# First samples in two pieces, with zero products between them, and another order of taps and weight sums, in a two-convolution transducer joint

## The chip, the cores and the metric

The kernel runs on one core of one Trainium2 chip. The metric is the device time of one execution in microseconds (us). A profile is one further execution of the same program. Its page and its trace count time from the first instruction of the program, and the span is the time from there to the end of the last one.

## The reference, cut to what matters

```python
B, T, D, K, U = 2, 4000, 512, 5, 8          # all inputs bf16
xp = pad(x, 2 samples of zeros at both ends of T)
h = sum(einsum("btc,cd->btd", xp[:, i:i+T, :], w1[i]) for i in range(K))
h = gelu(h)[:, ::2, :]                      # 2000 samples are kept
hp = pad(h, 2 at both ends)
f = sum(einsum("btc,cd->btd", hp[:, i:i+2000, :], w2[i]) for i in range(K))
f = gelu(f)[:, ::2, :]                      # 1000 samples are kept
fe, ge = f @ w_f, g @ w_g
j = tanh(fe[:, :, None, :] + ge[:, None, :, :])   # (2, 1000, 8, 512)
out = j @ w_o                               # bf16
```

The change touches the very start: the first convolution over the first samples of batch 0, and the sums of its weights that the rest of the convolution needs.

## The kernel before, in words

A small planner writes the program. Each operation is recorded with its engine, what it reads and writes and an estimated cost (`Plan.op`, `Plan.dma`). `schedule` then plays the operations through in time and settles the order in which each engine issues them, and `learn` repeats that up to `PASSES` times with other priorities, and keeps the best plan. Engines run their lists strictly in order and wait on semaphores. TensorE (PE) takes the ready operation that was recorded first; ScalarE (ACT) and VectorE (DVE) take the one with the least slack. All loads are issued by SyncE (SP), in the order of the record.

The work has these stages.

**Direct part.** For the first 444 kept samples of h in batch 0 the convolution is done tap by tap. `load_xr` brings the rows of x in, 128 partitions with two consecutive samples each (an even and an odd one), in four pieces `xr`: three of 256 KB and one of 128 KB. PE transposes each piece (lines 573 to 588): for each of the two phases, four 128x128 transposes into one PSUM bank. ACT copies the even phase, DVE the odd phase, into `eo`, which holds two phases of samples with channels on partitions. Then `direct(i)` (line 744) does the five taps in the order of `TAPS`, 16 products of 444 columns each: four output groups `m` of 128 channels, four slices of input channels. Even taps read the even phase of `eo`, odd taps the odd phase. The four groups accumulate in PSUM banks 0, 2, 4 and 6. While the first piece is on its way, `NWARM` products of zeros run on PE (`warm_mm`, line 565).

**Triple part.** The rest of the first convolution and all of the second one are done by `Triple` and `Unit`. Three neighbouring outputs are computed with nine products in place of fifteen, from sums and differences of samples (`row`, `xa`, `xp`) and of weights. The samples come by transposing DMAs (`load_x6`, line 513), six phases to a buffer. The weight sums are made by `w1part(m)` (line 612) for each of the four groups: seven sums on DVE, most with 512 elements on each partition, and three scaled copies on ACT. Groups m and m+2 share the scratch buffers `wu`, `ssum` and `ws`, so that group 2 can't be begun before group 0 has used them.

**Joint part.** `fe`, `ge`, tanh on ACT, and the last product with `w_o`, partly by a seven-product scheme (`Seven`), with stores by SP.

The order of SP's list at the start is: four `xr` pieces, tap 0 of `w1`; tap 2 (which waits until the third piece has landed); tap 4 (waits for the fourth piece); two transposing loads into `xa`; tap 1 (waits for tap 0); one `xa` load; tap 3 (waits for tap 2); three `xa` loads; then eighteen `xp` loads. The waits come from `came[-3]` in lines 535 to 541: a load may be issued when the third load before it in that list has landed.

Of the kernel before, what the change touches and what calls it, by code (L numbers as in the profile page):

```python
# [68 lines left out]
class Plan:  # L69
# [1 line left out]

    COMPUTE = ("pe", "act", "dve", "pool")
    HOP = 0.16
    PASSES = 100

    def __init__(self, nc):
        self.nc = nc
# [277 lines left out]
def bass_standalone__seq2seq_rnn_t_joint__speech_kernel(  # L355
# [22 lines left out]
    NK = D // P  # L378
# [3 lines left out]
    ND, NF = 444, 184  # L382
    NL = 2 * NT3 - ND // 3 - NF
    assert ND % 6 == 0 and NF % 2 == 0 and NL % 2 == 0
    EW = 464
    XW = 528
    HOFF, HWID = 2, 338
    JB = 2 * P
    RING, WIDE, XB = 12, 10, 24
    BU = B * U  # L390
    NT = 512
    NWARM = 5
    TAPS = (0, 2, 4, 1, 3)
    XR = [P] * ((ND + 1) // P) + [32 * -(-((ND + 1) % P) // 32)]
    NX = len(XR)

    with ExitStack() as es:
# [18 lines left out]
        wo_sb = at("wo_sb", [NK, D], BF16)  # L416
        h_off = cur[0]
        hT = [at(f"hT{b}", [6, NK, HWID], BF16) for b in range(B)]
        wu = [Buf(nc, f"wu{i}", [NK, P], FP32, h_off + 24576 + i * 2048) for i in range(2)]
        xr = [Buf(nc, f"xr{i}", [2, NK, P], BF16, h_off + 16384 + i * 2048) for i in range(NX)]  # L420
        assert hT[0].end <= h_off + 16384 and xr[-1].end <= h_off + 24576 and wu[1].end <= cur[0]
        sd = [at(f"sd{i}", [3, 336], FP32) for i in range(3)]
        ws = [at(f"ws{i}", [NK, P], FP32) for i in range(2)]
        ssum = [at(f"ssum{i}", [NK, P], FP32) for i in range(2)]
        geT = at("geT", [NK * BU], FP32)
        gT = at("gT", [NK, BU], BF16)
        zero = at("zero", [NT], BF16)
        ident = at("ident", [P], BF16)
# [1 line left out]
        xe = at("xe", [NK, 16], BF16)  # L430
        assert cur[0] <= 229368, cur[0]
        eo = Buf(nc, "eo", [2, NK, EW], BF16, w2_sb.end - w2_sb.bytes)
        assert eo.end <= w2_sb.end and 16 + sum(XR) <= EW
        xa = Buf(nc, "xa", [7, NK, 224], BF16, xs[0].end - xs[0].bytes)
        assert xa.end <= xs[0].end
        xp = [Buf(nc, f"xp{i}", [6, NK, 352], BF16, xs[i].end - xs[i].bytes) for i in range(3)]
        assert all(a.end <= b.end for a, b in zip(xp, xs))
        w1_x = Buf(nc, "w1_x", [3, NK, D], BF16, wf_sb.end - wf_sb.bytes)
# [34 lines left out]
        def tt(eng, o, a, b, op):  # L473
            pl.op(eng, lambda e: e.tensor_tensor(out=o.ap, in0=a.ap, in1=b.ap, op=op), (a, b), (o,),  # L474
                  0.02 + 2.14e-3 * o.ap.free_size() if eng == "pool" else vec_cost(o, (a, b)))

        def act(o, i, func, scale=1.0, bias=None):
            rd = (i,) if bias is None else (i, bias)
            pl.op("act", lambda e: e.activation(o.ap, i.ap, func, scale=scale,  # L479
                                                bias=0.0 if bias is None else bias.ap), rd, (o,),  # L480
                  o.ap.free_size() * 0.833e-3 + (0.05 if i.psum else 0.105 if bias is None else 0.186))

        def mm(o, pairs, start, stop, check=True):

            def fn(e):
                for n, (l, r) in enumerate(pairs):
                    ins = e.matmul(o.ap, lhsT=l.ap, rhs=r.ap, start=start and n == 0,  # L487
                                   stop=stop and n == len(pairs) - 1, skip_group_check=not check)
                return ins
            pl.op("pe", fn, [v for pr in pairs for v in pr], (o,), len(pairs) * max(o.ap.free_size() / 2400 + 0.0025, 0.1))  # L490


        zv = zero[:]
# [4 lines left out]
            out=idv.ap, in_=zero[0:P].ap, compare_op=ALU.not_equal, fill=1.0, base=0,  # L498
# [6 lines left out]
            return pl.dma(eng, lambda e: e.dma_start(dst.ap, src), (), (dst,), slack=slack)  # L505

        def load_xr(rt):
            n = XR[rt]
            dst = xr[rt].rows(0, n, slice(0, 2)).map(lambda a: a.rearrange("p r k c -> p (r k c)"))
            src = x[0, 2 * P * rt:2 * (P * rt + n), :].rearrange("(p r) c -> p (r c)", r=2)  # L510
            return pl.dma("sp", lambda e: e.dma_start(dst.ap, src), (), (dst,), nbytes=2048 * n)  # L511

        def load_x6(buf, b, ph, j0, col, n=336, slack=1.0):

            r0 = b * T + 6 * j0 + ph
            dst = buf[ph, :, col:col + n]
            src = x.rearrange("b t d -> (b t) d")[r0:r0 + 6 * (n - 1) + 1:6, :]
            return pl.dma("sp", lambda e: e.dma_start_transpose(out=dst.ap, in_=src), (), (dst,), nbytes=n * 2 * D, rate=175e3, slack=slack)  # L518
# [10 lines left out]
        JA, JL = ND // 3 - 1, (ND // 3 + NF) - 1  # L529

        def load_a(*phs):
            for ph in phs:
                load_x6(xa, 0, ph, JA, 0, 16 * -(-(NF + 2) // 16), 0.0)

        came.append(load_w1(TAPS[0]))
        for i in TAPS[1:3]:
# [7 lines left out]
        memset(xp[1][:, :, 336:340])  # L544
        pl.pin = False
        for ph in (4, 0, 2, 1, 3, 5):
            load_x6(xp[1], 0, ph, JL, 0, slack=0.3)
            if ph > 3:
                memset(xp[1][ph, :, 335:336])
        pl.pin = True  # L550
# [14 lines left out]
        def warm_mm(lo, hi):  # L565
            z, zz = zero[0:P], zero[:]
            for i in range(lo, hi):
                mm(ps.cols((2 * i + 1) % 8 * NT, NT), [(z, zz)], True, True)
                pl.ops[-1].cost = 0.43

        warm_mm(0, NWARM)
        psb = ps.h[:, :].bitcast(BF16)
        for rt in range(NX):
            for r in range(2):
                bk = (4 * rt + 2 * r) % 8
                n = XR[rt]
                pv = View(psb[:, bk * 1024:bk * 1024 + NK * n].rearrange("p (k c) -> p k c", k=NK), np.array([bk]), True)

                def fn(e, rt=rt, r=r, pv=pv, n=n):
                    for k in range(NK):  # L580
                        ins = e.transpose(pv.ap[:, k, :], xr[rt].h[0:n, r, k, :], ident.h[0:n, 0:n])
                    return ins
                pl.op("pe", fn, (xr[rt][:], ident[:]), (pv,), 0.43)
                o = eo[r, :, 16 + rt * P:16 + rt * P + n]
                if r == 0:
                    act(o, pv, ACT.Copy)
                else:
                    pl.op("dve", lambda e, o=o, pv=pv: e.tensor_copy(out=o.ap, in_=pv.ap), (pv,), (o,), vec_cost(o, (pv,)))

        def stt(eng, o, a, f, b):  # L590
            pl.op(eng, lambda e: e.scalar_tensor_tensor(  # L591
                out=o.ap, in0=a.ap, scalar=f, in1=b.ap, op0=ALU.mult, op1=add), (a, b), (o,),
                  vec_cost(o, (a, b), False))
# [18 lines left out]
        def w1part(m):  # L612
            sl = slice(m * P, (m + 1) * P)
            w = lambda i: w1_sb[i, :, sl]
            u, v, t = wu[m % 2][:], ssum[m % 2][:], ws[m % 2][:]
            stt("dve", u, w(4), 4.0, w(0))
            stt("dve", u, w(2), 2.0, u)
            act(w1_x[1, :, sl], u, ACT.Copy, scale=1.0 / 3.0)
            tt("dve", t, w(0), w(4), add)
            tt("dve", v, t, w(2), sub)  # L620
            act(w1_x[0, :, sl], v, ACT.Copy, scale=1.0 / 3.0)
            tt("dve", w1_t[2, :, sl], t, w(2), add)
            tt("dve", w1_x[2, :, sl], w(1), w(3), sub)
            tt("dve", w1_t[1, :, sl], w(1), w(3), add)
            act(w1_t[0, :, sl], w(1), ACT.Copy, scale=2.0)

        even, odd = [0, 2, 4, 6], [1, 3, 5, 7]

        class Triple:

# [112 lines left out]

        def direct(i):
            for m in range(NK):
                mm(ps.cols(2 * m * NT, ND),
                   [(w1_sb[i, k, m * P:(m + 1) * P], eo[i % 2, k, 15 + i // 2:15 + i // 2 + ND]) for k in range(NK)],
                   i == TAPS[0], i == TAPS[-1], False)

# [6 lines left out]
        for i in TAPS:  # L756
            direct(i)
        for m in range(NK):
            v = ps.cols(2 * m * NT, ND).map(lambda a: a.rearrange("p (q r) -> p r q", r=6))
            act(hT[0][:, m, HOFF:HOFF + ND // 6], v, ACT.Gelu_apprx_tanh)  # L760
        for m in range(NK):
            w1part(m)

        def load_rest():
            load_end()
# [126 lines left out]
        odd = free = even  # L892
# [165 lines left out]
        last0, cur = units[nu - 2], units[nu - 1]  # L1058
# [100 lines left out]
```

## Time and profile before

| What | Value |
|---|---|
| Median of 3 runs | 257.49 us (257.46 to 257.73) |
| The profiled execution | 257.44 us |
| Its span | 255.6 us |
| PE busy | 248.5 us, 97% of the span |
| ACT, DVE busy | 211.9 us, 207.0 us |
| First zero product on PE | 1.19 us |
| First product of the direct part | 8.07 us |
| First product of the triple part | 24.20 us |

The profiled execution takes 1.84 us more than its span, before the first instruction and behind the last one. In the page's part 2 each digit is the busy share of a fortieth of the span (6.4 us); in part 5 a group of like instructions has its busy time, the mean of one, and the idle time before them with what ended it. In the timeline a line has start and length in us, the engine, the line of the kernel, the operation, what it writes and reads with its shape, and, in brackets, the idle time before it and its releaser. A PE product's length there is the time until its last result; products overlap, so the distance from start to start is what one costs.

### The profile page before, as it was taken

The numbers are of one execution on the slowest core, as the hardware profiler recorded it, in microseconds if no ns is written. First come the engines' busy times: TensorE is split into PE (matmuls) and PEld (weight loads), VectorE is DVE, ScalarE is ACT, GpSimd is POOL, SyncE is SP. The second block draws the span as 40 slices with busy tenths as digits, with TensorE's granted clock in tenths as the row PEclk, the third lists the DMA queues.
The fourth block names the chain that finished last, engine by engine and source line by source line (L and its number), as shares of the span: only waits on it lengthen the run. The fifth ranks groups of instructions, "written<-read, shape, count | busy, mean of one in ns | idle before, by whom it ended". The sixth has DMA issues, their size and how long they took to land.

```text
span 255.6 us, 5244 instructions
## 1 busy us (share of the span) xinstructions
PE 248.5 (97%) x1901; PEld 180.0 (70%) x1901; DVE 207.0 (81%) x338; ACT 211.9 (83%) x356; POOL 102.6 (40%) x107
## 2 busy tenths in 40 slices
PE   6999989999999999999999999999999999999994
PEld 3555866666666666667557878877778877787882
DVE  1299999981999999198346889789899999989673
ACT  4296988839968767885499999999999999999862
POOL 1000000000000000000708899887796999998800
PEclk9999999999999999999999999999999999999999
DMA  6999999989100016000001322342235266454557
GB/s 186 271 243 176 192 168 178 165 169 359 30 0 0 3 35 211 4 1 3 0 0 46 121 82 86 107 141 85 83 126 174 75 197 215 162 179 158 172 160 226
DMA packets 55384, 31.87 MB, mean 125 GB/s; under 512 B 32094, under 2 KB 54910, under 8 KB 55358
## 3 DMA queue, kind: packets, MB, share of 16 engines
q1 hardware_dynamic: 55070, 31.34, 47.0%
q8 instruction: 15, 0.25, 0.5%
q10 hardware_dynamic: 288, 0.20, 0.2%
q14 instruction: 11, 0.09, 0.1%
HBM read 7.73 MB, written 16.38 MB: 94 GB/s over the span
## 4 chain that ended last, share of the span: by engine, by line
PE 81%; DVE 8%; DMA 4%; SPq 4%; issue 1%; ACT 0%; DVEq 0%
PE acc L487 81%; SPq L518 3%; DMA xa<-in_x_dram 2%; DVE row L474 2%; DMA xr<-in_x_dram 2%; DVE xp L474 1%; DVE w_t L474 1%; DVE xa L474 1%; DVE wu L591 1%; SPq L505 1%; DVE ssum L474 1%; SPq L511 0%; DVE ws L474 0%; DVE acc L591 0%; DVE sd L474 0%
## 5 line engine op out<-in xcount | busy, mean ns | idle before, releaser
L474 DVE TENSOR_TENSOR og<-acc,sn 128x512 bf16<-128x512 f32 x84 | 55.5, 682 | 9.7 <-PE acc L487 7.7
L479 ACT ACTIVATE jT<-feT,geT 128x1000 bf16<-128x1000 f32 (+6 forms) x56 | 52.6, 1025 | 0.5 <-DVE feT L794 0.4
L487 PE MATMUL acc<-tw,ss 128*128 128x256 f16 x336 | 46.3, 273 | 0.0
L487 PE MATMUL acc<-row,w_sb 128*128 128x334 bf16 (+2 forms) x224 | 38.9, 296 | 0.1
L901 ACT ACTIVATE sn<-acc 128x512 f32<-128x512 f32 x55 | 36.5, 676 | 2.6 <-PE acc L487 1.7
L487 PEld LDWEIGHTS acc<-tw,ss 128*128 128x128 f16 x336 | 32.5, 98 | 7.7 <-ACT sn L901 0.2
L964 POOL TENSOR_TENSOR ss<-jT 128x512 f16<-128x512 bf16 x24 | 29.4, 1235 | 12.8 <-ACT jT L479 10.4
L487 PE MATMUL acc<-wo_sb,jT 128*128 128x256 bf16 (+1 forms) x192 | 32.1, 295 | 0.0
L487 PEld LDWEIGHTS acc<-row,w_sb 128*128 128x128 bf16 x224 | 20.9, 97 | 9.2 <-DVE acc L591 0.6
L479 ACT ACTIVATE jX<-feT,geT 128x1000 bf16<-128x1000 f32 (+4 forms) x28 | 26.9, 1029 | 0.0
L591 DVE SCALAR_TENSOR_TENSOR acc<-acc,sd 128x334 f32<-128x334 f32 (+2 forms) x24 | 11.6, 482 | 15.6 <-PE acc L487 15.6
L479 ACT ACTIVATE sd<-acc 128x334 f32<-128x334 f32 (+2 forms) x48 | 19.9, 433 | 4.5 <-PE acc L487 3.3
L487 PEld LDWEIGHTS acc<-wo_sb,jT 128*128 128x128 bf16 x192 | 18.7, 98 | 6.2
L479 ACT ACTIVATE hT<-acc 128x334 bf16<-128x334 f32 (+3 forms) x36 | 15.2, 436 | 9.1 <-PE acc L487 8.8
L471 POOL MEMSET hT<- 128x8 bf16 (+2 forms) x6 | 0.8, 147 | 54.6 <-ACT hT L479 47.3
L902 DVE COPY sn<-acc 128x512 f32<-128x512 f32 x29 | 19.7, 682 | 1.3 <-PE acc L487 1.0
L964 POOL TENSOR_TENSOR ss<-jT,ss 128x512 f16<-128x512 bf16 x16 | 18.8, 1179 | 0.8 <-DVE ss L964 0.4
L474 DVE TENSOR_TENSOR row<-row 128x1336 bf16<-128x1336 bf16 (+2 forms) x24 | 19.0, 793 | 0.0
L487 PE MATMUL acc<-hT,w_t 128*128 128x334 bf16 x96 | 17.6, 304 | 0.0
L487 PE MATMUL acc<-xp,w_t 128*128 128x334 bf16 (+1 forms) x96 | 17.4, 305 | 0.0
L487 PE MATMUL acc<-wo_sb,ss 128*128 128x256 bf16 x112 | 17.0, 273 | 0.0
L487 PE MATMUL acc<-xp,w_x 128*128 128x334 bf16 (+1 forms) x96 | 16.9, 305 | 0.0
(108 smaller groups left out, 508.7 us busy)
## 6 DMA issues: line engine op xcount, KB each, us to landing
out_dram<-og SPq DMA_DIRECT2D x98, 128.0 KB, 2.0
w_sb<-in_w_dram SPq DMA_DIRECT2D x10, 512.0 KB, 5.1
out_dram<-ost SPq DMA_DIRECT2D x10, 128.0 KB, 2.2
xr<-in_x_dram SPq DMA_DIRECT2D x3, 256.0 KB, 3.0
wf_sb<-in_w_f_dram SPq DMA_DIRECT2D x1, 512.0 KB, 3.7
wg_sb<-in_w_g_dram SPq DMA_DIRECT2D x1, 512.0 KB, 4.7
wo_sb<-in_w_o_dram SPq DMA_DIRECT2D x1, 512.0 KB, 5.6
xp<-in_x_dram SPq DMA_TRANSPOSE x18, 5.0
```

Of the source, the lines that this page charges most:

```text
L471: pl.op("pool", lambda e: e.memset(v.ap, 0.0), (), (v,))
L474: pl.op(eng, lambda e: e.tensor_tensor(out=o.ap, in0=a.ap, in1=b.ap, op=op), (a, b), (o,), 0.02 + 2.14e-3 * o.ap.free_size() if eng == "po ...
L479: pl.op("act", lambda e: e.activation(o.ap, i.ap, func, scale=scale, bias=0.0 if bias is None else bias.ap), rd, (o,), o.ap.free_size() * ...
L487: ins = e.matmul(o.ap, lhsT=l.ap, rhs=r.ap, start=start and n == 0, stop=stop and n == len(pairs) - 1, skip_group_check=not check)
L505: return pl.dma(eng, lambda e: e.dma_start(dst.ap, src), (), (dst,), slack=slack)
L518: return pl.dma("sp", lambda e: e.dma_start_transpose(out=dst.ap, in_=src), (), (dst,), nbytes=n * 2 * D, rate=175e3, slack=slack)
L591: pl.op(eng, lambda e: e.scalar_tensor_tensor(out=o.ap, in0=a.ap, scalar=f, in1=b.ap, op0=ALU.mult, op1=add), (a, b), (o,), vec_cost(o, (a ...
L901: pl.flex({"act": (lambda e: e.activation(o.ap, v.ap, ACT.Copy), 0.05 + n * 0.833e-3), "dve": (lambda e: e.tensor_copy(out=o.ap, in_=v.ap) ...
L902: "dve": (lambda e: e.tensor_copy(out=o.ap, in_=v.ap), 0.065 + n * 1.04e-3)}, (v,), (o,))
L964: fn = lambda e, o=S[i], x=x, y=y, op=op: e.tensor_tensor(out=o.ap, in0=x.ap, in1=y.ap, op=op)
```

## The change

- `xr` comes in two pieces of 512 KB, four consecutive samples on each partition, 1 MB in all (896 KB before).
- PE transposes the even phase of both pieces first and the odd phase after it. Each 128 columns of a transposed piece go into `eo` with a step of two columns. DVE and ACT have changed places: samples 0 and 1 of a partition's four go through DVE, 2 and 3 through ACT.
- Seven products of zeros (five before) run ahead of the first piece, and two more between the first and the second piece.
- The taps go in the order 0, 4, 2, 1, 3. The waits of SP keep their rule, so tap 4's load now waits for the first piece and tap 2's for the second.
- The four groups of the direct part stand in banks 4, 6, 0 and 2.
- `w1part` is cut in two: what needs taps 0 and 4 alone is recorded for all groups first, the rest after it. Each group has its own `wu` and `wv` buffers; `ssum` is still shared by pairs.
- The planner's costs for PE and for some loads are changed, and it makes up to 150 passes (100 before), so the order of other operations moves too.

In the changed program the starts of the lists are these. PE: 7 zero products; 8 transposes of piece 1 (even); 2 zero products; 8 transposes of piece 2 (even); 4 transposes of piece 1 (odd); tap 0, group 0; 4 transposes of piece 1 and 4 of piece 2 (odd); tap 0, groups 1 and 2; the last 4 transposes of piece 2 (odd); tap 4, groups 0 and 1; then the rest. DVE: three copies into `eo`; two sums of group 0, from taps 0 and 4; the last copy into `eo`; six more sums of groups 0 and 1; and so on.

```diff
-    PASSES = 100
+    PASSES = 150
...
-    NWARM = 5
-    TAPS = (0, 2, 4, 1, 3)
-    XR = [P] * ((ND + 1) // P) + [32 * -(-((ND + 1) % P) // 32)]
-    NX = len(XR)
+    NWARM = 7
+    TAPS = (0, 4, 2, 1, 3)
+    NX = 2
...
-        xr = [Buf(nc, f"xr{i}", [2, NK, P], BF16, h_off + 16384 + i * 2048) for i in range(NX)]
+        xr = [Buf(nc, f"xr{i}", [4, NK, P], BF16, h_off + 16384 + i * 4096) for i in range(NX)]
...
+        wv = ws + [at(f"wv{i}", [NK, P], FP32) for i in range(2)]
...
-            src = x[0, 2 * P * rt:2 * (P * rt + n), :].rearrange("(p r) c -> p (r c)", r=2)
-            return pl.dma("sp", lambda e: e.dma_start(dst.ap, src), (), (dst,), nbytes=2048 * n)
+            src = x[0, 4 * P * rt:4 * P * (rt + 1), :].rearrange("(p r) c -> p (r c)", r=4)
+            return pl.dma("sp", lambda e: e.dma_start(dst.ap, src), (), (dst,), rate=370e3)
...
+        for pp in range(2):
+            for rt in range(NX):
+                for r in range(2):
+                    bk = 2 * rt if pp else 4 * rt + 2 * r
+                    lo = bk * 1024 + pp * r * 512
...
+                    if not pp and not rt and r:
+                        warm_mm(NWARM, NWARM + 2)
+                    lo = 16 + 2 * P * rt + r
+                    o = eo[pp, :, lo:lo + 2 * P - 1:2]
+                    if r:
+                        act(o, pv, ACT.Copy)
+                    else:
+                        pl.op("dve", lambda e, o=o, pv=pv: e.tensor_copy(out=o.ap, in_=pv.ap), (pv,), (o,), vec_cost(o, (pv,)))
...
+            u, v, t = wu[m][:], ssum[m % 2][:], wv[m][:]
+            if part == "04":
+                stt("dve", u, w(4), 4.0, w(0))
+                tt("dve", t, w(0), w(4), add)
+            else:
+                stt("dve", u, w(2), 2.0, u)
...
-                mm(ps.cols(2 * m * NT, ND),
+                mm(ps.cols((4 + 2 * m) % 8 * NT, ND),
...
         for m in range(NK):
-            w1part(m)
+            w1part(m, "04")
+        for m in range(NK):
+            w1part(m, "213")
```

More of the change, by code (lines that the diff above doesn't have):

```diff
@@ L384, in bass_standalone__seq2seq_rnn_t_joint__speech_kernel @@
     assert ND % 6 == 0 and NF % 2 == 0 and NL % 2 == 0
-    EW = 464
+    EW = 16 + 4 * P
     XW = 528
@@ L418, in bass_standalone__seq2seq_rnn_t_joint__speech_kernel @@
         hT = [at(f"hT{b}", [6, NK, HWID], BF16) for b in range(B)]
-        wu = [Buf(nc, f"wu{i}", [NK, P], FP32, h_off + 24576 + i * 2048) for i in range(2)]
-        xr = [Buf(nc, f"xr{i}", [2, NK, P], BF16, h_off + 16384 + i * 2048) for i in range(NX)]
-        assert hT[0].end <= h_off + 16384 and xr[-1].end <= h_off + 24576 and wu[1].end <= cur[0]
+        xr = [Buf(nc, f"xr{i}", [4, NK, P], BF16, h_off + 16384 + i * 4096) for i in range(NX)]
+        assert hT[0].end <= h_off + 16384 and xr[-1].end <= h_off + 24576
         sd = [at(f"sd{i}", [3, 336], FP32) for i in range(3)]
         ws = [at(f"ws{i}", [NK, P], FP32) for i in range(2)]
+        wv = ws + [at(f"wv{i}", [NK, P], FP32) for i in range(2)]
+        wu = [Buf(nc, f"wu{i}", [NK, P], FP32, h_off + 24576 + i * 2048) for i in range(3)] + [at("wu3", [NK, P], FP32)]
+        assert wu[2].end <= sd[0].end - sd[0].bytes
         ssum = [at(f"ssum{i}", [NK, P], FP32) for i in range(2)]
@@ L432, in bass_standalone__seq2seq_rnn_t_joint__speech_kernel @@
         eo = Buf(nc, "eo", [2, NK, EW], BF16, w2_sb.end - w2_sb.bytes)
-        assert eo.end <= w2_sb.end and 16 + sum(XR) <= EW
+        assert eo.end <= w2_sb.end and ND < 4 * P
         xa = Buf(nc, "xa", [7, NK, 224], BF16, xs[0].end - xs[0].bytes)
@@ L489, in fn @@
                 return ins
-            pl.op("pe", fn, [v for pr in pairs for v in pr], (o,), len(pairs) * max(o.ap.free_size() / 2400 + 0.0025, 0.1))
+            pl.op("pe", fn, [v for pr in pairs for v in pr], (o,), len(pairs) * max(o.ap.free_size() / 2400 + 0.0028, 0.056))
         zv = zero[:]
@@ L507, in load_xr @@
         def load_xr(rt):
-            n = XR[rt]
-            dst = xr[rt].rows(0, n, slice(0, 2)).map(lambda a: a.rearrange("p r k c -> p (r k c)"))
-            src = x[0, 2 * P * rt:2 * (P * rt + n), :].rearrange("(p r) c -> p (r c)", r=2)
-            return pl.dma("sp", lambda e: e.dma_start(dst.ap, src), (), (dst,), nbytes=2048 * n)
+            dst = xr[rt][:].map(lambda a: a.rearrange("p r k c -> p (r k c)"))
+            src = x[0, 4 * P * rt:4 * P * (rt + 1), :].rearrange("(p r) c -> p (r c)", r=4)
+            return pl.dma("sp", lambda e: e.dma_start(dst.ap, src), (), (dst,), rate=370e3)
         def load_x6(buf, b, ph, j0, col, n=336, slack=1.0):
@@ L532, in load_a @@
             for ph in phs:
-                load_x6(xa, 0, ph, JA, 0, 16 * -(-(NF + 2) // 16), 0.0)
+                load_x6(xa, 0, ph, JA, 0, 16 * -(-(NF + 2) // 16), 0.8)
         came.append(load_w1(TAPS[0]))
@@ L546, in bass_standalone__seq2seq_rnn_t_joint__speech_kernel @@
         for ph in (4, 0, 2, 1, 3, 5):
-            load_x6(xp[1], 0, ph, JL, 0, slack=0.3)
+            load_x6(xp[1], 0, ph, JL, 0, slack=1.2)
             if ph > 3:
@@ L572, in bass_standalone__seq2seq_rnn_t_joint__speech_kernel, with fn @@
         psb = ps.h[:, :].bitcast(BF16)
[L573 to L588, printed above, removed]
+        for pp in range(2):
[3 more added lines that the diff above has]
+                    lo = bk * 1024 + pp * r * 512
+                    pv = View(psb[:, lo:lo + 512].rearrange("p (k c) -> p k c", k=NK), np.array([bk]), True)
+                    def fn(e, rt=rt, pp=pp, r=r, pv=pv):
+                        for k in range(NK):
+                            ins = e.transpose(pv.ap[:, k, :], xr[rt].h[:, 2 * r + pp, k, :], ident.h[:, :])
+                        return ins
+                    pl.op("pe", fn, (xr[rt][:], ident[:]), (pv,), 0.22 if pp and rt else 0.43)
+                    if not pp and not rt and r:
[6 more added lines that the diff above has]
+                        pl.op("dve", lambda e, o=o, pv=pv: e.tensor_copy(out=o.ap, in_=pv.ap), (pv,), (o,), vec_cost(o, (pv,)))
         def stt(eng, o, a, f, b):
@@ L610, in w2part, with w1part @@
                 act(w(1), w(1), ACT.Copy, scale=2.0)
-        def w1part(m):
+        def w1part(m, part):
             sl = slice(m * P, (m + 1) * P)
             w = lambda i: w1_sb[i, :, sl]
[L615 to L627, printed above, removed]
+            u, v, t = wu[m][:], ssum[m % 2][:], wv[m][:]
[4 more added lines that the diff above has]
+                stt("dve", u, w(2), 2.0, u)
+                act(w1_x[1, :, sl], u, ACT.Copy, scale=1.0 / 3.0)
+                tt("dve", v, t, w(2), sub)
+                act(w1_x[0, :, sl], v, ACT.Copy, scale=1.0 / 3.0)
+                tt("dve", w1_t[2, :, sl], t, w(2), add)
+                tt("dve", w1_x[2, :, sl], w(1), w(3), sub)
+                tt("dve", w1_t[1, :, sl], w(1), w(3), add)
+                act(w1_t[0, :, sl], w(1), ACT.Copy, scale=2.0)
+        even, odd = [4, 6, 0, 2], [1, 3, 5, 7]
         class Triple:
@@ L758, in bass_standalone__seq2seq_rnn_t_joint__speech_kernel @@
         for m in range(NK):
-            v = ps.cols(2 * m * NT, ND).map(lambda a: a.rearrange("p (q r) -> p r q", r=6))
+            v = ps.cols((4 + 2 * m) % 8 * NT, ND).map(lambda a: a.rearrange("p (q r) -> p r q", r=6))
             act(hT[0][:, m, HOFF:HOFF + ND // 6], v, ACT.Gelu_apprx_tanh)
         for m in range(NK):
-            w1part(m)
+            w1part(m, "04")
+        for m in range(NK):
+            w1part(m, "213")
         def load_rest():
```

## The prediction

> **What bounds the kernel now.** I read the chain of work that ended last first, then busy time by windows, then the timeline of the first 45 us engine by engine, then landings.
>
> The chain in order of time, read from its end:
>
> ```profile
> 15.26 5.92 DMA xa<-in_x_dram
> 21.19 0.02 issue
> 21.21 1.01 DVE xa L474 x2
> ...
> 43.64 0.52 DVE acc L591
> 44.16 0.05 issue
> 44.21 207.97 PE acc L487 x1600
> 252.18 0.02 issue
> 252.20 0.38 ACT ost L479
> ```
>
> From 44.21 us PE runs on without a break to 252.18; the stores behind it end the span at 255.6. From 21.2 to 44.2 the chain lies on DVE. The windows say the same (columns: stretch, its length, busy time of PE, PEld, DVE, ACT, POOL, then clock, DMA share and GB/s):
>
> ```profile
> 24.20:44.20 20.00, 18.71 (x185) 14.63 (x183) 19.96 (x39) 18.19 (x35) 0.70 (x5) 1.00 1.08 178
> 44.20:252.20 208.00, 207.96 (x1600) 153.89 (x1600) 172.76 (x272) 180.31 (x300) 100.73 (x89) 1.00 0.36 107
> ```
>
> DVE is full from 24.2 to 44.2, and PE isn't. From start to start a PE product of 184 columns takes 0.079 us there and one of 336 takes 0.143; 144 and 40 of them are 17.1 us of work in 20.0, so PE loses 2.9 us: the waits for DVE that the timeline shows at 33.2, 36.5, 37.6, 40.3 and 43.8 come to about 1.6, those for ACT at 25.1, 26.7, 27.7 and 31.3 to about 1.1. So **the time is set by when DVE is through its load at 43.6**, and an earlier PE alone gains nothing. Now the start:
>
> ```profile
> 3.57 1.89 PE L581 MATMUL acc<-ident,xr 128*128 128x128 bf16 x16
> ...
> 6.25 1.55 PE L581 MATMUL acc<-ident,xr 128*128 128x128 bf16 x16 [0.80 <-DMA xr<-in_x_dram]
> ...
> 8.07 14.23 PE L487 MATMUL acc<-eo,w_sb 128*128 128x444 bf16 x69 [0.26 <-ACT eo L479]
> ...
> 9.90 0.15 PEld L487 LDWEIGHTS acc<-eo,w_sb 128*128 128x128 bf16 x1 [0.22 <-issue]
> 10.27 11.78 PEld L487 LDWEIGHTS acc<-eo,w_sb 128*128 128x128 bf16 x63 [0.22 <-issue]
> ...
> 11.73 0.69 DVE L591 SCALAR_TENSOR_TENSOR wu<-w_sb 128x512 f32<-128x512 bf16 x1 [3.59 <-DMA w_sb<-in_w_dram]
> ```
>
> DVE idles 3.59 us and starts the weight sums at 11.73, when the third tap has landed (issued 6.72, 5.0 to landing). PE waits 0.80 us for the third piece of x and starts the taps at 8.07. Until 10.27 its products are 0.37 us apart, behind that 0.188 (11.78 over 63): it ran at half speed, and 6 products cost 1.1 us more than later ones. The page's clock row shows 9 throughout and doesn't tell this.
>
> **First product (T0).** The loads now come as 1 MB of x and 0.5 MB of tap 0, one behind the other. Half-microsecond windows of before show 385 GB/s at 2.5 and some 260 from 3.5 to 6; they add up to 0.52 MB at 3.7 us, 1.05 MB at 5.9. Landings lag the bytes by about 0.6 (tap 4: last bytes at 11.1, landed 11.71). So piece 1 is in at 4.2 (the second of the old pieces, the same bytes, was in at 1.19 + 3.0) and piece 2 at 6.5; bounds 5.7 (all of it at 385 GB/s) and 7.1 (the last old piece, 0.9 MB, landed at 2.12 + 4.58 = 6.70; 0.13 MB more at 260 add 0.5). Tap 0 landed at 2.74 + 5.1 = 7.82; behind 0.13 MB more it is 8.3. From piece 2, eight transposes and the second copy: before, the third piece's second copy started 1.05 behind the transposes' start (6.25, 7.30), and an ACT copy takes 0.60: 6.5 + 1.05 + 0.60 + 0.06 = 8.2. T0 is 8.3, bounds 7.6 and 9.0. The seven zero products (0.427 apart, from 1.19) end at 4.2 and the two others fit between 5.1 and 6.0: they cost nothing, because PE waits for x there; if x came sooner, they would cost up to 0.85.
>
> **PE up to the triples.** 80 products at 0.188 are 15.04. PE is only idle some 0.5 us ahead of T0, against 0.80 + 0.26 before, so I take full speed from the first product on; bounds 0 and 1.1 us for that, the row's own loss. Twelve transposes now lie behind T0, at 0.053 apart (the row at 7.20): 0.64. The last four wait for the DVE copy that is queued behind two weight sums, which wait for tap 4. Its load is issued when piece 1 is in (4.3, before 6.72) and flows right behind tap 0: 8.3 + 0.52 MB at 385 = 9.7. Two sums (0.60 apart on DVE) and the copy (0.42) end at 11.4; PE comes there at 8.3 + 12 x 0.188 + 8 x 0.053 = 11.0 and waits 0.4. Behind it on PE is everything. PE reaches the triples at 8.3 + 15.04 + 0.64 + 0.4 = 24.4 (24.2 before): **nothing is gained on PE itself**, and at full speed it would pass the old 44.2 at 24.4 + 17.1 = 41.5, plus up to 1.1 of ACT's waits.
>
> The copy's columns now have a step of two. The nearest row is the old copy, 0.42, and I take that; 0.68, as the sums with 512 elements in f32, is the other end. By the Trainium skill, VectorE: DVE Perf Modes, section "Mode 2×_1P — pack two bf16 into one 32-bit read", the double rate needs 16-bit data with a step of one, so the copy would lose it; by that the train below is 0.26 longer and the time 0.26 later; no run here shows it yet.
>
> **DVE, which decides.** It starts at 9.7 in place of 11.73. Two sums and the copy: 11.5. Tap 2 (issued at 6.5, behind tap 4 on the wire) is in at 9.7 + 1.4 = 11.1. Six sums, 3.6: 15.1. Then a `row` difference (0.46) and three sums (1.8): 17.4. The next `row` waits for ACT's scaled copy of the third `xa` phase. ACT's list ahead of it now has five scaled weight copies of 0.6 and three `row` steps of 0.75 from 12.2 on, with 0.6 for one more weight copy and a short wait: it is done at 18.2 (18.12 before), and DVE loses 0.8. From 18.2: `row`, sum, `row`, a weight difference, `xa`, two `row`s, two weight differences (0.46 + 0.60 + 0.46 + 0.33 + 0.46 + 0.92 + 0.66 = 3.9) reach 22.1; the two `xa` differences need loads that landed at 21.2 before, so no wait: 23.0. Before, DVE had done at 22.80 the same without two sums (1.2). Lead: 1.2 - 0.2 = 1.0 us. Nothing behind that is added; the `xp` loads land 4 us or more ahead of use (the last of the first six at 33.3, used at 39.5). So PE's free run starts at 43.2, later than its own 41.5 + 1.1: DVE still sets it.
>
> **Sum.** 44.2 - 1.0 = 43.2; plus the unbroken rest, 255.6 - 44.2 = 211.4: span 254.6, and with the 1.84 outside it **256.4 us** (257.44 for the profiled execution before, 257.49 the median, the same within 0.05). The later order is replanned too; PE's waits behind 44.2 come to 0.3 in all, so +-0.3 for that.
>
> **The rivals.**
> (B) ACT is not in the way and weight sums keep the whole lead: 11.73 - 9.7 - 0.4 = 1.6, and up to 2.2 if x comes at 385 GB/s. For it: DVE's idle time of 3.59. Against it: ACT's busy 4.98 of 5 us from 15 to 20. 255.4.
> (C) The clock: PE stays at half speed until 10.27. Half of 8.3 to 10.27, 1.0, is lost, less the 0.4 wait: triples at 25.0, and 42.1 + 1.1 = 43.2 is a tie with DVE; with some of both, 256.8. For it: the idle time ahead of piece 2 may be as long as before. The Trainium skill's TensorE: Matmul & The Clock Gate, Part 1, has the clock open after a busy window of some 3.4 us that runs free of the kernel's start; by that the step at 10.27 could fall anywhere from run to run, which speaks against this gain as a fixed one, while three runs within 0.27 us here speak against much play.
> (D) Slower: loads come late. Two 512 KB pieces must land whole, tap 4 with them; if tap 4 lands at L, DVE's copy ends at L + 1.7, PE stands before the last four transposes until then, and DVE has a copy more to do behind the wait. From L = 11.3 (11.73 less 0.4) the lead is gone; at L = 12 the result is +0.7, 258.2. For it: the old pieces 3 and 4 landed 4.5 and 4.6 us behind their issue against 2.8 for the first, and rates fell to 199 GB/s at 5. Against it: tap 2 and tap 4 were then held back by SP's waits until 6.1 and 6.7, and the wire was down to 51 GB/s from 7.5 to 8.0; that hole is filled now.
> (E) The change does nothing: what DVE gains at 9.7 it waits out for `xa` landings (21.2) and ACT, 257.4.
>
> **Chances and range.** Forecast 0.46 (256.0 to 256.9), B 0.20, C 0.08, E 0.14, D 0.12. Faster by over 0.2% (0.5 us, about what a measurement of this kernel can tell from no change) is the forecast, B and C, 0.74; within 0.2% E, 0.14; slower D, 0.12. Range 255.1 to 257.9: B with the earliest loads at the low end; at the high end the copy at 0.68, the clock and half of D.
>
> **What would show it.** In the profile after: first product at 8.3 (7.6 to 9.0) and 0.188 apart at once; first weight sum on DVE at 9.7, not 11.73; a PE wait of about 0.4 at the last transposes, ended by DVE; the `row` difference behind it ended by ACT near 18.2; triples at 24.4; PE unbroken from 43.2, with the rest 211.4 as before. It is wrong if tap 4 lands behind 11 us, or if PE is not held by DVE between 30 and 43.

## The result, and the profile after

The changed kernel takes **254.9 us** (254.82 to 255.36), the kernel before, measured beside it, 257.48 (256.68 to 257.73): ratio 0.9909, interval 0.9884 to 0.9933. That is 1.5 us below the forecast and 0.2 below the low end of its range. The profiled execution took 254.9 with a span of 253.1 (before 257.44 and 255.6). One run of the kernel before that stands beside e1 to e4 (260.67) was a slow one: the ratios leave it out, the medians do not.

The chain of waits of the changed kernel, near its end (start, length, what):

```profile
31.54 0.46 issue
32.00 0.43 DVE w_x L475
32.48 98.84 PE acc L488 x710
```

PE's unbroken run begins at 32.48; before it began at 44.21. The stretch from 24.2 to 44.2 of the changed kernel (columns as in the prediction):

```profile
24.20:44.20 20.00, 19.83 (x201) 16.66 (x199) 19.78 (x36) 18.94 (x38) 0.36 (x3) 1.00 1.05 182
```

PE is busy 19.83 of 20 us where it was 18.71. DVE is as full as before (19.78), and yet no longer holds PE. The start on PE, changed kernel:

```profile
4.21 1.03 PE L582 MATMUL acc<-ident,xr 128*128 128x128 bf16 x8
5.03 0.64 PE L488 MATMUL acc<-zero 128*128 128x512 bf16 x2
5.50 0.83 PE L582 MATMUL acc<-ident,xr 128*128 128x128 bf16 x12
7.76 0.91 PE L488 MATMUL acc<-eo,w_sb 128*128 128x444 bf16 x4 [1.43 <-DMA w_sb<-in_w_dram]
8.52 0.61 PE L582 MATMUL acc<-ident,xr 128*128 128x128 bf16 x8
8.96 1.71 PE L488 MATMUL acc<-eo,w_sb 128*128 128x444 bf16 x8
10.97 0.40 PE L582 MATMUL acc<-ident,xr 128*128 128x128 bf16 x4 [0.30 <-DVE eo L592]
11.21 12.95 PE L488 MATMUL acc<-eo,w_sb 128*128 128x444 bf16 x68
23.99 1.12 PE L488 MATMUL acc<-xa,w_x 128*128 128x184 bf16 x12
```

All transposes that fit are done by 6.3; PE then waits for tap 0, not for x. The four products from 7.76 are 0.19 apart: full speed (the clock steps up at 5.1 us, before at 10.28). The last transposes wait for a DVE copy, 0.47 from start to start beyond a product. DVE at its start:

```profile
8.99 0.69 DVE L595 SCALAR_TENSOR_TENSOR wu<-w_sb 128x512 f32<-128x512 bf16 x1 [1.73 <-DMA w_sb<-in_w_dram]
9.60 0.68 DVE L475 TENSOR_TENSOR ws<-w_sb 128x512 f32<-128x512 bf16 x1
10.20 0.72 DVE L592 COPY eo<-acc 128x512 bf16<-128x512 bf16 x1
```

Tap 4 is in at 8.96, and the weight sums start at 8.99 (before 11.73).

**Where 2.55 us of span went.** First product of the direct part 8.07 to 7.76: -0.31. From there to the triples: +0.10, in which a clock gain of 1.1 is used up by twelve transposes (0.64) and the copy wait (0.47). From the triples (24.20, now 23.99) to the first product of the second convolution (95.37, now 93.06): -2.10. From there to the last product 156.5 in both. The tail: -0.25. So most of the gain lies in waits of PE between 24 and 44, 2.85 us before and 0.63 now (start-to-start distances beyond 0.0795 and 0.143, summed from the first product of the triples to 45 us).

### The profile page after: what moved, and what is told of

It is laid out like the page before. It is cut to its first block, busy times and chain, and to the rows that moved or that the text cites. A ratio compares the mean times of both kernels' runs of the same rounds, so it can differ in the third digit from the quotient of the medians.

```text
span 253.1 us, 5249 instructions
## 1 busy us (share of the span) xinstructions
PE 246.5 (97%) x1899; PEld 180.1 (71%) x1905; DVE 210.4 (83%) x342; ACT 210.6 (83%) x352; POOL 103.1 (41%) x107
## 4 chain that ended last, share of the span: by engine, by line
PE 85%; DVE 8%; DMA 3%; issue 2%; ACT 0%; DVEq 0%
PE acc L488 85%; DMA w_sb<-in_w_dram 2%; DVE wu L595 2%; DVE row L475 2%; DMA xr<-in_x_dram 1%; DVE xa L475 1%; DVE ssum L475 1%; DVE w_t L475 1%; DVE og L475 1%; DVE ws L475 0%; DVE w_x L475 0%; DVE sd L475 0%; DVE wv L475 0%; DVE eo L592 0%; DVE acc L595 0%
## 5 line engine op out<-in xcount | busy, mean ns | idle before, releaser
L909 ACT ACTIVATE sn<-acc 128x512 f32<-128x512 f32 x54 | 34.6, 654 | 3.8 <-PE acc L488 3.5
L972 POOL TENSOR_TENSOR ss<-jT 128x512 f16<-128x512 bf16 x23 | 28.8, 1263 | 13.4 <-ACT jT L480 10.8
L488 PE MATMUL acc<-wo_sb,jT 128*128 128x256 bf16 (+1 forms) x187 | 31.5, 292 | 0.3
L480 ACT ACTIVATE jX<-feT,geT 128x1000 bf16<-128x1000 f32 (+4 forms) x28 | 26.2, 983 | 0.0
L910 DVE COPY sn<-acc 128x512 f32<-128x512 f32 x30 | 20.5, 685 | 2.5 <-PE acc L488 2.4
L972 POOL TENSOR_TENSOR ss<-jX 128x512 f16<-128x512 bf16 x15 | 17.4, 1169 | 1.1 <-ACT jX L480 0.6
L488 PE MATMUL acc<-eo,w_sb 128*128 128x444 bf16 x80 | 15.6, 351 | 1.4 <-DMA w_sb<-in_w_dram 1.4
```

The source lines that it names most:

```text
L909: pl.flex({"act": (lambda e: e.activation(o.ap, v.ap, ACT.Copy), 0.05 + n * 0.833e-3), "dve": (lambda e: e.tensor_copy(out=o.ap, in_=v.ap) ...
L910: "dve": (lambda e: e.tensor_copy(out=o.ap, in_=v.ap), 0.065 + n * 1.04e-3)}, (v,), (o,))
L972: fn = lambda e, o=S[i], x=x, y=y, op=op: e.tensor_tensor(out=o.ap, in0=x.ap, in1=y.ap, op=op)
```

## The experiments

"Waits" is that sum; it, the first weight sum on DVE and the first product of the triples are from the profiled run (us). The kernel before was run beside every group of kernels. Chips are numbered as the results name them. The profiled execution is one of the runs and not always near the median: it is the longest of e7, e8, e10 and e12, and the shortest or next to it of e1 and e2.

| Run | Edit | Median, us (lowest to highest) | Before, same chip | Ratio, interval | First sum | Triples | Waits |
|---|---|---|---|---|---|---|---|
| e1 | changed kernel (chip 5) | 254.94 (254.60 to 255.57) | 258.41 | 0.9875 (0.984 to 0.991) | 8.75 | 23.76 | 0.57 |
| e2 | without long rows | 256.13 (255.35 to 257.70) | 258.41 | 0.9925 (0.9896 to 0.9953) | 9.62 | 24.63 | 0.66 |
| e3 | old tap order | 255.79 (255.58 to 255.90) | 258.41 | 0.9904 (0.987 to 0.9938) | 10.77 | 23.98 | 1.66 |
| e4 | zero products cut short | 256.47 (255.52 to 257.03) | 258.41 | 0.9931 (0.9905 to 0.9958) | 8.80 | 25.73 | 0.34 |
| e5 | before + two zero products (chip 9) | 257.09 (256.32 to 258.86) | 257.85 | 0.997 (0.9942 to 0.9998) | 12.07 | 23.02 | 3.97 |
| e6 | before + tap order | 257.93 (256.50 to 259.35) | 257.85 | 0.9985 (0.9955 to 1.0015) | 9.61 | 24.71 | 2.38 |
| e7 | odd transposes in own banks | 254.51 (254.24 to 254.71) | 257.85 | 0.9854 (0.9822 to 0.9885) | 9.35 | 23.21 | 1.06 |
| e8 | even samples loaded first | 257.51 (256.40 to 258.63) | 257.85 | 0.9974 (0.9948 to 1.0) | 8.81 | 27.64 | 0.55 |
| e9 | before + both of e5 and e6 (chip 6) | 257.37 (256.12 to 258.44) | 258.04 | 0.9974 (0.9946 to 1.0002) | 9.62 | 22.83 | 3.90 |
| e10 | e7 again | 254.33 (254.04 to 254.65) | 258.04 | 0.9845 (0.981 to 0.988) | 9.39 | 23.25 | 1.11 |
| e11 | changed kernel | 254.91 (254.63 to 255.09) | 258.04 | 0.9868 (0.9837 to 0.99) | 8.77 | 23.78 | 0.65 |
| e12 | old planner numbers (chip 3) | 257.78 (256.71 to 259.66) | 258.44 | 0.9976 (0.9941 to 1.001) | 9.87 | 24.28 | 3.20 |

**e1 and e11: the changed kernel itself**, as the measure beside the others.

> The changed kernel once more, as the mark for the three kernels that run beside it on the same chip. All theories: 254.9 us, 2.5 below the kernel before, and in the profile the first weight sum on DVE near 9.0 us and the triples from 24.0 us. What may differ from run to run is the moment at which PE goes to full speed: if it is bound to the kernel's start it lies at 5.1 us again, if it runs free it lies anywhere.

> The changed kernel unaltered, as the measure for the two others on this chip: 254.5 to 255.3.

It gives 254.9 on each of the chips that it ran on, with little spread. The kernel before spreads from 256.4 to 260.2. The clock stepped up at 5.24 in e1 and at 4.67 in e11, so that moment moves.

**e2: without long rows.** Each piece comes as two loads of 256 KB with rows of 2 KB; the rest of the program is the same, and DVE and ACT go through their lists in the same order.

```diff
-            dst = xr[rt][:] ... (r=4), rows of 4 KB
+            for r in (0, 2):
+                dst = xr[rt][r:r + 2] ...
+                src = x[...].rearrange("(p r) c -> p r c", r=4)[:, r:r + 2] ...
```

> The same program, but each 512 KB piece comes as two loads of 256 KB with rows of 2 KB on a partition in place of one with rows of 4 KB. Theory (the rows' length made the wire faster, about 400 GB/s from 3 to 4.5 us against 260 before): piece 2 lands near 6.5 in place of 5.4, tap 0 near 8.3 in place of 7.5, tap 4 near 9.8 in place of 9.0; then DVE starts 0.8 later, and the time is 255.4 to 255.8. Rival (the length is of no account, the order of the loads alone counts): landings as in the changed kernel and 254.9.

Tap 4 is in at 9.6 in place of 8.7, the sums start 0.9 later, and the median is 1.2 higher, a little more than the theory gave. What the DMA engines moved, changed kernel:

```profile
2.50:4.50 2.00, 2.00 (x9) 0.68 (x7) 0.00 (x0) 0.00 (x0) 0.00 (x0) 1.00 0.99 399
4.50:8.00 3.50, 2.07 (x23) 1.54 (x22) 2.06 (x3) 1.48 (x2) 0.00 (x0) 1.00 1.01 343
```

and e2, same windows:

```profile
2.50:4.50 2.00, 1.85 (x5) 0.39 (x3) 0.00 (x0) 0.00 (x0) 0.00 (x0) 1.00 0.93 268
4.50:8.00 3.50, 1.90 (x22) 1.23 (x22) 1.61 (x3) 0.80 (x2) 0.00 (x0) 1.00 0.98 325
```

The last column is GB/s, the one before it the busy share of the DMA engines: nearly as busy, they bring fewer bytes with 2 KB rows. But 2 KB rows are not always as slow: in the window from 2.5 to 4.5 the kernel before has 320, and e5, e6 and e9, which load like it, 374 to 379. e2 also issues two loads more, so that tap 0 goes out at 2.60 in place of 1.65. The length of the rows and the number of loads were not run apart.

**e3: the old tap order in the changed kernel** (`TAPS = (0, 2, 4, 1, 3)`).

> The changed kernel with the taps in the old order 0, 2, 4, 1, 3. Theory (the gain is DVE's early start on the weight sums): tap 4 lands 1.9 later, near 10.8, the first sum moves there, a good part of PE's waits for DVE between 25 and 43 us comes back, 256.0 to 256.6. Rival (the gain is PE's start and its clock): PE has its first product at 7.8 and full speed all the same, 254.9 to 255.2.

DVE's first sums, e3:

```profile
10.77 0.69 DVE L595 SCALAR_TENSOR_TENSOR wu<-w_sb 128x512 f32<-128x512 bf16 x1 [0.41 <-DMA w_sb<-in_w_dram]
```

They start 2.0 later than in e1, the waits in the triples grow by 1.1, and the median by 0.85: between what the theory and the rival gave. The planner also orders the lists of DVE and ACT anew here, so that not all of it need be the taps.

**e4: the nine zero products cut to 2 columns**, at the same places.

```diff
-                mm(ps.cols((2 * i + 1) % 8 * NT, NT), [(z, zz)], True, True)
+                mm(ps.cols((2 * i + 1) % 8 * NT, 2), [(z, zero[0:2])], True, True)
```

> The changed kernel with all nine zero products cut from 512 columns to 2, so that PE is idle where it was filled; the order of every engine stays. Theory (the clock is worth little): PE goes to full speed later, at 8 to 10.3, and what is slow lies partly in waits that are there anyway (1.4 for tap 0, 0.5 for the last copy); 255.0 to 255.8. Rival (the clock is the gain): the whole of it goes, 256.5 or more. If the moment of full speed runs free, the runs spread by up to 1 us.

PE, e4:

```profile
7.69 1.66 PE L488 MATMUL acc<-eo,w_sb 128*128 128x444 bf16 x4 [0.80 <-DVE eo L592]
9.15 1.06 PE L582 MATMUL acc<-ident,xr 128*128 128x128 bf16 x8
10.00 2.88 PE L488 MATMUL acc<-eo,w_sb 128*128 128x444 bf16 x8
```

Four products take 1.66 where the changed kernel needs 0.91: half speed, until 12.45. The triples come 1.97 later than in e1, and the median is 1.5 higher, which is the rival's figure and not the theory's. The zero products are worth that much here, because PE, not DVE, now sets the end: the waits that could have hidden it are down to 0.34.

**e5 and e6: the two small edits, each alone in the kernel before.** In e5 two zero products are put between the second and the third piece (`if rt == 2: warm_mm(NWARM, NWARM + 2)`); in e6 the taps go 0, 4, 2, 1, 3.

> The kernel before with two more zero products between its second and third piece of x, and nothing else; the order of every engine is the same. Theory (before the change DVE sets the end of the triple part, so that an earlier clock of PE is worth little there): PE goes to full speed 3 us or so earlier and reaches the triples up to 1.1 us sooner, but waits for DVE the longer; the time is 0 to 0.3 below the kernel before. Rival (the clock carries over as in the changed kernel, where its loss cost 1.5): 1.0 to 1.5 below the kernel before, and less spread from run to run.

> The kernel before with the taps in the order 0, 4, 2, 1, 3, and nothing else. Theory (DVE's start decides): the load that DVE waits for lands near 10.1 in place of 11.7, and the time falls by 0.8 to 1.4. Rival (the loads' speed and PE's clock carry the gain): no change, within 0.3.

In e5 the clock opens at 5.63 and the triples begin 1.2 earlier (23.02), but the second convolution at 95.31, as before (95.37). PE waits the gain out (3.97 us in the triples, 2.85 before), as the theory had it; the median is 0.8 below that of before, more than the theory's 0.3 and less than the rival's 1.0. The stretch from 24.2 to 44.2 in e5:

```profile
24.20:44.20 20.00, 18.32 (x177) 14.02 (x178) 19.97 (x39) 17.96 (x34) 0.69 (x5) 1.00 1.09 173
```

In e6 DVE starts 2.1 earlier, and nothing comes of it: the rival's figure. Part of that is a half-speed window in the profiled run. The window from 8 to 12 us of e6, with the clock at 0.57:

```profile
8.00:12.00 4.00, 4.00 (x13) 1.72 (x14) 2.18 (x4) 0.00 (x0) 0.00 (x0) 0.57 0.99 262
```

So e5 and e6 left it open whether the two need each other.

**e9: both in the kernel before.**

> The kernel before with both small edits at once: the tap order 0, 4, 2, 1, 3, and two zero products between the second and the third piece. No long rows, no other transposes, no other buffers. Theory (the two gains need each other: DVE's lead counts only where PE comes early, and PE's early start only where DVE has a lead; in each edit alone one of them was waited out): triples from 22.8 to 23.2, first weight sum on DVE by 9.8, waits of PE in the triples 0.6 to 1.6 us, first product of the second convolution at 92.6 to 94.0 where the kernel before has 95.4, median 254.7 to 256.0. Rival (without the 4 KB rows nothing much comes of it): 256.2 to 257.5, waits of PE in the triples over 2 us.

The theory fell. The triples begin at 22.83 and the first sum at 9.62, as it wanted, but PE waits 3.90 us in the triples, the second convolution starts at 95.05, and the median is 0.7 below that of before, an interval that reaches no change. The stretch from 24.2 to 44.2 in e9:

```profile
24.20:44.20 20.00, 17.66 (x174) 13.88 (x172) 19.65 (x37) 17.21 (x33) 0.61 (x5) 1.00 1.07 176
```

and in e2, where DVE starts at the same 9.62:

```profile
24.20:44.20 20.00, 19.83 (x201) 16.59 (x199) 19.78 (x38) 19.08 (x38) 0.36 (x3) 1.00 1.07 175
```

DVE is equally full in both, but PE is busy 17.66 us in e9 and 19.83 in e2. (Some of e9's fewer products in the window were done ahead of it, because its triples begin 1.80 earlier.) For all that early start, e9 begins the second convolution 1.3 later than e2, at 95.05 against 93.73. The two differ in the order (e9's is that of e6), but also in the buffers of the weight sums, which bind the order, and in their loads: tap 3 lands at 19.04 in e9 and at 17.25 in e2. The next run takes the order alone.

**e12: the changed kernel with the planner's old numbers.**

```diff
-            ... len(pairs) * max(o.ap.free_size() / 2400 + 0.0028, 0.056))
+            ... len(pairs) * max(o.ap.free_size() / 2400 + 0.0025, 0.1))
...
-            load_x6(xa, 0, ph, JA, 0, ..., 0.8)
+            load_x6(xa, 0, ph, JA, 0, ..., 0.0)
...
-            load_x6(xp[1], 0, ph, JL, 0, slack=1.2)
+            load_x6(xp[1], 0, ph, JL, 0, slack=0.3)
```

(and the cost of an `xr` load by its bytes in place of a rate)

> The changed kernel with the planner's old numbers: the cost of a PE product (0.0025 and a least value of 0.1 in place of 0.0028 and 0.056), the slack of the xa and xp loads (0.0 and 0.3 in place of 0.8 and 1.2) and no rate for the x loads. Work, loads, taps, zero products and buffers are the changed kernel's; only the order that the planner finds differs, on PE, DVE and ACT. Theory (the plan is a part of the gain, and what e9 lacked; e2 had the changed plan and DVE's start of e9, and its waits were 0.7 where e9 had 3.8): 255.6 to 256.8, waits of PE in the triples 1.5 to 3.0 us where the changed kernel has 0.65. Rival (the long rows, the tap order and the zero products do it, whatever the plan): 254.6 to 255.3, waits under 1.2.

It takes 257.78, 2.9 above the changed kernel on the other chips and near the kernel before, past the upper end of what the theory gave. PE in the triples, e12, the groups with a marked wait (2.1 of the 3.2 us):

```profile
25.83 0.49 PE L488 MATMUL acc<-row,w_x 128*128 128x184 bf16 x4 [0.43 <-ACT sd L480]
...
28.12 0.49 PE L488 MATMUL acc<-row,w_t 128*128 128x184 bf16 x4 [0.20 <-ACT sd L480]
...
30.15 0.49 PE L488 MATMUL acc<-row,w_sb 128*128 128x184 bf16 x4 [0.26 <-DVE acc L595]
...
31.17 0.49 PE L488 MATMUL acc<-row,w_sb 128*128 128x184 bf16 x4 [0.21 <-DVE sd L475]
...
34.88 0.49 PE L488 MATMUL acc<-row,w_sb 128*128 128x184 bf16 x4 [0.35 <-DVE acc L595]
...
40.57 0.74 PE L488 MATMUL acc<-row,w_t 128*128 128x336 bf16 x4 [0.63 <-ACT sd L480]
```

PE waits for small steps that empty PSUM and merge sums, `sd` and `acc`. DVE in e12, the two first merges and the point at which DVE set the end before (43.64 there):

```profile
28.80 0.68 DVE L475 TENSOR_TENSOR ssum<-wv,w_sb 128x512 f32<-128x512 f32 x1
29.41 0.41 DVE L475 TENSOR_TENSOR w_x<-w_sb 128x512 bf16<-128x512 bf16 x1
29.74 0.35 DVE L595 SCALAR_TENSOR_TENSOR acc<-acc,sd 128x184 f32<-128x184 f32 x1
...
31.03 0.34 DVE L595 SCALAR_TENSOR_TENSOR acc<-acc,sd 128x184 f32<-128x184 f32 x1
...
42.00 0.50 DVE L595 SCALAR_TENSOR_TENSOR acc<-acc,sd 128x336 f32<-128x336 f32 x1
```

and in the changed kernel:

```profile
28.31 0.35 DVE L595 SCALAR_TENSOR_TENSOR acc<-acc,sd 128x184 f32<-128x184 f32 x1
28.57 0.42 DVE L475 TENSOR_TENSOR w_t<-w_sb 128x512 bf16<-128x512 bf16 x1
28.90 0.34 DVE L475 TENSOR_TENSOR sd<-acc,sd 128x184 f32<-128x184 f32 x1
29.16 0.35 DVE L595 SCALAR_TENSOR_TENSOR acc<-acc,sd 128x184 f32<-128x184 f32 x1
...
41.42 0.52 DVE L595 SCALAR_TENSOR_TENSOR acc<-acc,sd 128x336 f32<-128x336 f32 x1
```

At 42.00 DVE in e12 is 1.64 us ahead of before, and PE gains nothing: the second convolution starts at 95.87. The merges come 1.4 and 1.9 us later than in the changed kernel, behind weight sums; 0.9 of that is tap 4, which landed at 9.85 here and at 8.96 there. e2 gives the same comparison without that: there tap 4 landed at 9.60, DVE started at 9.62 and the triples at 24.63 (e12: 9.87 and 24.28), PE's waits were 0.66 in place of 3.20, and the second convolution started at 93.73 in place of 95.87. So an order that fits is worth about 2 us of waits in the triples. Why the old numbers give a worse order is argued, not shown. The old least value of 0.1 counts each of the 144 products of 184 columns at 0.1 where the trace has 0.079, so the planner took PE to be up to 144 x 0.021 = 3.0 us later than it is; that may be why it put merges behind sums. Which of the numbers does it was not run, nor were they tried in the kernel before alone. The profiled execution of e12, its longest (259.66), also has a wait of 1.9 us in the joint part, at 216 us; its shortest, 256.71, is still 2.1 above the shortest of e11. Its lists differ from the changed kernel's in the joint part too, so that not all of the 2.9 need lie in the triples.

**e7 and e10: the odd transposes in PSUM banks of their own.**

```diff
-                    bk = 2 * rt if pp else 4 * rt + 2 * r
-                    lo = bk * 1024 + pp * r * 512
+                    bk = 4 * rt + 2 * r + pp
+                    lo = bk * 1024
```

> The changed kernel with the odd phase's transposes in PSUM banks 1, 3, 5 and 7 of their own, so that all of them run in the wait for tap 0 and no product waits for a copy: 12 transposes (0.64) and the wait of 0.5 go from PE's path ahead of the triples. Theory (PE sets the time in the changed kernel, with 0.6 us of waits for DVE and ACT left): 0.5 to 1.0 below the changed kernel, 253.9 to 254.4. Rival (DVE, which is busy without a break from 23.4 to 41, takes over at once): 0 to 0.3 below, 254.6 to 254.9.

> The changed kernel with the odd transposes in PSUM banks of their own once more, beside the changed kernel on the same chip. Theory (the 0.6 us that the banks keep PE from standing behind a copy are a gain of their own): 0.2 to 0.7 below the changed kernel's median. Rival (the earlier difference was one chip's, or the moment at which the clock opens): within 0.2.

PE, e10:

```profile
5.89 1.91 PE L582 MATMUL acc<-ident,xr 128*128 128x128 bf16 x24
8.18 15.23 PE L488 MATMUL acc<-eo,w_sb 128*128 128x444 bf16 x80 [0.38 <-ACT eo L480]
23.25 0.96 PE L488 MATMUL acc<-xa,w_x 128*128 128x184 bf16 x10
```

All transposes stand ahead of tap 0, for the most part in time that PE waited for it anyway, and the 80 products run without a break. On one chip e10 takes 254.33 and the changed kernel 254.91, and the ranges only just meet (254.65 and 254.63). This beats both kernels, by 0.6 and 3.7 us. e7's 254.51 lay between its theory and its rival. In the profiled runs, 254.65 and 254.86, the triples begin 0.53 earlier, but the waits there grow from 0.65 to 1.11: most of a further gain on PE is waited out again. Where the rest of the 0.6 between the medians lies is open.

**e8: even samples first.** As e7, with the even samples of both pieces in two loads of 256 KB (rows of 1 KB), the odd ones loaded behind tap 2 and transposed between taps 4 and 2.

```diff
-        came = [load_xr(rt) for rt in range(NX)]
+        came = [load_xr(rt, 0) for rt in range(NX)]
...
+            if i == 2:
+                transposes(1)
```

> As the kernel with odd banks, and the even samples of both pieces (2 x 256 KB, rows of 1 KB) are loaded ahead of tap 0, the odd ones behind tap 2; the odd phase is transposed between taps 4 and 2. Theory (the start hangs on the bytes ahead of tap 0, 1.0 MB in place of 1.5): tap 0 lands near 6.0 in place of 7.5, the first product at 6.2, tap 4 near 7.3; PE reaches the triples 1 us sooner than with odd banks and DVE has as much more lead: 252.9 to 253.8. Rival (the loads of samples for the triples, behind the same bytes as before, or DVE, end the gain): 254 to 254.6; and rows of 1 KB may run at 260 GB/s as those of 2 KB did.

Half of the bytes, and the second piece is in at 5.69, no sooner than all of it with 4 KB rows (5.43). The odd samples land at 13.21, PE stands 2.05 us in the direct part from 17.88 on and runs nine products behind it at half speed (1.7 more), and the triples begin at 27.64. That is the longest run of e8. The expectation failed on the short rows at the start (first product at 7.78, not 6.2) and on the odd samples, which it did not have coming late.

**Two parts that change nothing.** With the weight sums recorded group by group, as before, the planner writes the same order for every engine; with 100 passes it writes the same program as with 150. Neither was run.

## Why the prediction was right and wrong

Right: faster, and the cost of most single steps. Wrong: the size, 1.0 us forecast in place of 2.5, and the reason.

- **First product.** 8.3 forecast, 7.76 measured. The mis-sized term is the loads: piece 2 at 6.5, measured 5.43, and tap 0 at 8.3, measured 7.52, because I carried 260 GB/s over from 2 KB rows. e2, which has such rows, has them at 6.64 and 8.22.
- **Full speed from the first product:** right. The reason given, little idle time on PE, was not: PE stood 1.43 us ahead of it and kept its clock.
- **Twelve transposes at 0.64 and a wait of 0.4:** 0.64 and 0.47. **Triples** at 24.4: 23.99, by the earlier start.
- **The copy:** 0.42 taken, 0.73 measured. The other end, 0.68, was nearly right, and so was the Trainium skill, VectorE: DVE Perf Modes, section "Mode 2×_1P — pack two bf16 into one 32-bit read": with a step of two the double rate is lost.
- **DVE** starts at 8.99, not 9.7 (tap 4 comes behind the same loads). The `row` difference behind ACT started at 17.87, forecast 18.2, and the wait of 0.8 for ACT ahead of it did not come: DVE has no idle time there. DVE's first merge of 336 columns, the one that set the end before, comes at 41.42 against 43.64, a lead of 2.2 where 1.0 was forecast.
- **The step that failed:** "PE's free run starts at 43.2 ... DVE still sets it", with "the later order is replanned too ... +-0.3". It took DVE's lead as PE's gain, one for one, and the order as given. PE did that work in the changed kernel by 23.99 + 17.2 + 0.63 = 41.8, not by 43.2. In the one profiled execution of each, e12, e9 and e6 have leads of 1.64, 1.66 and 1.30 at the same merge and start the second convolution 0.50 later, 0.32 earlier and 0.05 later than the kernel before; e10 has a lead of 1.56 and starts it 2.63 earlier. e5 has no lead, and its gain on PE is lost. PE is held not by the end of DVE's load but by small steps on the way, copies out of PSUM on ACT and merges on DVE, and their place in the lists comes from the planner. By the prediction's own sign, PE held by DVE between 30 and 43, it was wrong: the changed kernel has one such wait of more than 0.1 us there, 0.25 ahead of 32.48. I read "DVE full from 24.2 to 44.2" as "DVE is the bound"; it is nearly as full in the changed kernel (19.78), while PE waits 0.63 us in all.
- **The rest unchanged:** 156.5 and 156.5. Right.

The rivals: B's figure (255.4) came nearest, its lead of 1.6 to 2.2 too, but with the same wrong link. C, the clock, was forecast at a loss of 0.4 to the result; in the changed kernel it is worth 1.5 (e4, where full speed came at 12.45). By the Trainium skill, TensorE: Matmul & The Clock Gate, Part 1, the window runs free of the kernel's start, and the runs agree: the clock opened anywhere between 3.98 and 6.74 in the eleven profiled runs with full zero products between the pieces, and within one trace its steps lie whole multiples of 3.41 us apart (10.28 and 256.04 before: 72 of them). D did not come: tap 4 landed at 8.96. E's time is what e9 and e12 came to, but not by its way: their DVE kept a lead, and PE lost it in waits.

Taken out of the changed kernel, the planner's numbers cost 2.9, the zero products 1.5, the long rows 1.2, the tap order 0.85: 6.4 in all, about twice the 3.1 to 3.5 by which the changed kernel beats the kernel before on the same chips. That they come to more than the whole fits parts which need one another: an early PE, an early DVE and an order in which the merges come in time. What the planner's numbers do alone in the kernel before stays open; so does why the kernel before and e12 spread over 3 to 4 us and the changed kernel over 1.

## What to carry to other kernels

A full engine is not yet the bound: look which instruction the other one waits for, and whether it stands in the list behind work that nobody needs yet. Where a planner orders the work, its numbers can eat all that earlier data brings (e12), so compare its costs with start-to-start times of the trace (0.1 against 0.079 here), and count a replan as a term of its own. Test gains together as well as alone.

## What the runs showed of the hardware

- From 2.5 to 4.5 us the eight traces with rows of 4 KB show 389 to 416 GB/s, the five with rows of 2 KB 268 (e2), 320 (before) and 374 to 379 (e5, e6, e9), with the DMA engines busy 0.93 to 1.10 in all of them; half the bytes in 1 KB rows (e8) landed no sooner.
- A PSUM copy to bf16 with a step of two took 0.73 on DVE (0.42 without) and 0.74 on ACT (0.60).
- Products of zeros open the clock like any others: 5.1 against 12.45 with short ones (e4). An idle time of 1.43 us (changed kernel, 6.33 to 7.76) did not close it. In e6, where PE stood 1.35 and 0.69 us between 5.57 and 7.99, the clock fell to half for one window, from 8.19 to 11.60; in e8, behind the wait of 2.05 us, from 21.05 to 24.46.
- The length of a wait alone does not decide it: e3 stands 2.04 us, from 6.19 to 8.23, and keeps its clock. Cut into windows of 3.41 us that end where the clock steps, PE's busy share at the start tells the cases apart. It was 40% in the windows behind which the clock fell (e6, 4.78 to 8.19; e8, 17.64 to 21.05) and 45% in one behind which it held (e3, 4.67 to 8.08). From half speed it did not rise behind windows of 75% (before, 3.45 to 6.86) and 77% (e4, 5.62 to 9.04), and it rose behind one of 82% (e8, 0.57 to 3.98). These are shares of these traces, and a PE product's end in them is modelled.
